# Landmark sums of two batches gated and halved, and a new spacing of the planned attention steps

## The chip, the cores and the metric

One NeuronCore of a Trainium2 chip runs the whole program. Its engines are TensorE (PE, with its weight loads as PEld), VectorE (DVE), ScalarE (ACT), GpSimd (POOL) and the queue of SyncE (SP), which issues DMAs. The metric is the device time of one execution in microseconds; for the kernel before, the median of three runs is 846.47 us (845.29 to 849.52).

## What is computed

A Nystrom attention over 4 batches of 8 heads (576 positions, head size 64, 32 landmarks) feeds two feed-forward layers over 2304 tokens (512 to 2048 to 512).

```
q_lm = q.reshape(B, H, 32, 18, D).mean(axis=3)      # k_lm likewise
A = sm(q, k_lm); Bm = sm(q_lm, k_lm); C = sm(q_lm, k)
Z = Bm.T / (norm1(Bm) * norminf(Bm) + 1e-6)
for _ in range(6):
    Z = 2 * Z - Z @ Bm @ Z
x = A @ Z @ C @ v                 # heads side by side: 2304 x 512
h = x @ w_in1;  x = (h * clip(h + 3, 0, 6) / 6) @ w_out1
h = x @ w_in2;  out = elu(h) @ w_out2
```

The landmark sums are the sums over 18 positions in the first line.

## The kernel before

**Slots.** The first feed-forward layer is cut into 128 slots: 4 batches (b = 0 to 3 in the code, batches 1 to 4 in this text) of 32 slots, each one half of a batch's tokens by one of 16 blocks of the hidden layer. `slot_a1(i)` (line 876) makes the first product of slot i, six matmuls into a tile h (from the tiles ath, atl, nh, nl), then ACT and VectorE make gf from it, ACT gh, and GpSimd or VectorE gl. `slot_a2(i)` (line 906) makes the second product, four groups (one for each dm) of three matmuls into the tiles x. In one turn the first product of slot i and the second of slot i - 3 are made. From slot 32 on a half has 288 tokens. There are two PSUM banks for h, so the h matmuls of slot i + 2 wait until VectorE has read h of slot i.

**Attention.** While the slots of one batch run, the attention of the next is worked in between them, on all engines, as Python generators that give up control after each step: landmark sums (`prep`, line 469, letters p and P for the two groups of heads), score products and their softmax (c: `score_c`, b: `score_b`), the softmax over landmarks (a: `soft`), the iteration for Z (i: `inverse`), the products with v (v, V: `values`), and the end (f: `finish`, with the tiles t0 and Qd on VectorE, a matmul, and a copy; t: `attn_at`). `prep` reduces the tile kt, and then qt into the tile lm, with one VectorE instruction each (128 x 1152 elements to 128 x 64). `score_c` is, in this order: the first half of the products (bk from kt and lm), ACT copies of it into kt, the second half of the products, the row maxima on VectorE in two steps, the exponentials. `inverse` is: VectorE work (BD, BT), two kinds of matmuls, VectorE work that ends with X, then matmuls from X and a VectorE update of X in turn.

**What sets the order.** For batch 2 it is written by hand: in the string PLAN1 (line 1139) each letter s advances the stream of slots by one step (one yield per slot up to slot 15, five per slot from 16 to 35: after the six h matmuls and after each of the four groups), and every other letter one attention step; here each engine's order is the traced one. For batches 3 and 4 it is the string PLAN2 (line 708): `newton(b, at, end)` (line 733) spreads its due times, scaled so that the last is reached at slot `end`, over slots 36 to 56.5 (batch 3) and 64 to 88.5 (batch 4). In the main loop (line 1203) `attend(t)` carries out all steps due up to t, at t = i, and i + 0.2 to i + 0.8 between the groups of slot i. From the end of batch 2's attention on, a scheduler that simulates the program picks the order on each engine by a priority (`wanted`) among what it holds to be ready, so that an engine that it holds to be idle also takes later work. Matmuls of attention (`amm`) and of slots (`smm`) keep their traced order on TensorE through edges. An edge by `after` (so also by `gated`) orders the scheduling alone and is no semaphore on the chip. In the last stage (slots 96 to 127) no attention is left; VectorE and ACT split operands of the second layer there (`load_x`, `load_in2`), and conversions of weights (`conv_out2`, `conv_in2`) run beside the slots throughout.

Of the kernel before, what the change touches and what calls it, by code (L numbers as in the profile page):

```python
# [31 lines left out]
def nystrom_ffn_kernel(ctx: ExitStack, tc, q, k, v, w_in1, w_out1, w_in2, w_out2, out):  # L32
# [117 lines left out]
    def wanted(s):  # L150
        tc.cur_priority = int(1000 * (s + 100))
# [11 lines left out]
    def gated(inst):  # L163
        if gate[0] is not None:
            after(inst, gate[0])
# [84 lines left out]
    def run(gen):  # L250
        for _ in gen:
            pass
# [216 lines left out]
    def prep(b, g):  # L469

        x = kt_t[b, g] = raw_t.pop((b, g, "k"))
        y = qt_t[b, g] = raw_t.pop((b, g, "q"))
        lm = ql_t[b, g] = ap_.tile([128, 2, 32], F32, name="lm", tag="lm", bufs=2)
        for o, i in ((x[:, :, 0:32], x[:, :, 32:]), (lm, y)):
            gated(vec.tensor_reduce(
                out=o, in_=i.rearrange("p r (l c) -> p r l c", c=POOL), axis=AX, op=ALU.add
            ))
            yield 1.3

    def products(ps, w, x, gs):  # L480

# [219 lines left out]
    def newton_tiles():  # L701
# [4 lines left out]
        return EB, sb, sc, cvs  # L706

    PLAN2 = """
        p0 p2 P4 P6 c10 b11 b12 c12.5 c15 c15.5 c16.5 c17.5 i18 i21 i22 i24 i25 a26 a27 i30 i31
        a32 a33 i36 i37 v38 v39 v41 i43.5 i44.5 v45 a45.2 v46 i47 i48 a48.5 V50 V51 V53 a53.5 i55  # L710
        i56 V57 i57.2 a57.5 V58 a59 a60 t60.5 f61 f62 t62.5 f64 f65 t65.5
    """

    def attention(b):
# [18 lines left out]
    def newton(b, at, end):  # L733

        make, gens = attention(b), {}
        plan = PLAN2.split()
        unit = (end - at) / float(plan[-1][1:])
        for x in plan:
            s = at + unit * float(x[1:])
            yield s  # L740
            if x[0] not in gens:
                gens[x[0]] = make[x[0]]()
            wanted(s)
            next(gens[x[0]], None)
        for x in gens.values():
            run(x)
        yield 10 ** 9
# [128 lines left out]
    def slot_a1(i):  # L876
        b, hf, m = i // SB, i // NKT % 2, i % NKT
        nt = span(b, hf)[1]
        ps = banks["h"].tile([128, 512], F32, name="h", tag="h")[:, 0:nt]
        c, o = m // MPC, m % MPC * 128  # L880
        nh, nl = n_t[b, c]
        ath, atl = at_t[b, hf]
        n = 0
        for g in range(G):
            for w, x in ((nh, atl), (nl, ath), (nh, ath)):
                marks["slot"] = smm(ps, w[:, g, o:o + 128], x[:, g, :], n == 0, n == 3 * G - 1).ins
                n += 1
        gf = ft.tile([128, T2], F32, name="gf", tag="gf", bufs=2)[:, 0:nt]
        yield
        act.activation(out=gf, in_=ps, func=AF.Relu, scale=1.0 / 6.0, bias=half_b)  # L890
        yield
        if i < NKT:
            g = gp.tile([128, T2], F32, name="g", tag="gh")[:, 0:nt]
            vec.scalar_tensor_tensor(out=g, in0=gf, scalar=1.0, in1=ps, op0=ALU.min, op1=ALU.mult)
            gt[i] = g, None
            return
        gh = gp.tile([128, T2], F32R, name="gh", tag="gh")[:, 0:nt]
        gl = gp.tile([128, T2], F32R, name="gl", tag="gl")[:, 0:nt]
        vec.scalar_tensor_tensor(out=gf, in0=gf, scalar=1.0, in1=ps, op0=ALU.min, op1=ALU.mult)
        yield  # L900
        act.copy(out=gh, in_=gf)
        yield
        sub(gl, gf, gh.bitcast(F32), vec if i >= NA - 12 else pool)
        gt[i] = (gh, gl)
# [231 lines left out]
                yield  # L1136
            run(a2)

    PLAN1 = "ssssssuulslullslsssspsspssPssPsssoscsbsbcssosccscscsiosssiosissisiosasasssisisasasssisiosvsvososvssisisvasvsisiassVsVsosVassisisVoiasVosasassssosssffftftsssstosnTssnossnosnsssnsTsnosssnsssTssssssss"

    def second_half(slots):

# [60 lines left out]
    for i in range(END, NA):  # L1203
        b, r = i // SB, i % SB

        wanted(i)
        if r == 0:
            run(attn_n(b, NW - 1))
            run(attn_at(b, 1))
            if b + 1 < B:  # L1210
                soon, ready[0] = newton(b + 1, i, i + SB - 7.5), i
            else:
                att.close()
                win.append(ctx.enter_context(tc.tile_pool(name="win", bufs=1, side="right", reuse_waits="tile")))
                xp.append(win[0])
                x0 = load_x(0, vec)
        if b + 1 < B and r in NAT:
            run(attn_n(b + 1, NAT.index(r)))
        if (i - END) % O2 == 0 and conv:
            gate[0] = marks["slot"]  # L1220
            wanted(i + 4)
            conv.pop(0)()
            gate[0] = None
        if i >= NA - SB + XSET:
            wanted(i + 4)
            next(x0, None)
        if i == NA - 14:
            wanted(i + 2)
            load_in2(0)
        attend(i)  # L1230
        a1, a2 = slot_a1(i), slot_a2(i - DELAY)
        next(a1)
        for dm in range(NDM):
            attend(i + (dm + 1) / (NDM + 1))
            next(a1, None)
            next(a2)
        run(a1)
        run(a2)
# [78 lines left out]
```

## Time and profile before

| what | value |
|---|---|
| median of 3 runs | 846.47 us (845.29 to 849.52) |
| profiled execution | 848.42 us |
| its span on the core | 846.6 us |
| TensorE busy | 789.4 us (93%) |
| VectorE busy | 513.9 us (61%) |
| ACT busy | 449.7 us (53%) |
| GpSimd busy | 327.2 us (39%) |
| mean granted clock of TensorE | 0.985 |

In that execution slot 16 starts at 94 us, slot 36 at 172, slot 64 at 267, slot 96 at 367 and slot 127 at 451; the second layer follows. A row of a timeline gives start and duration in us, engine, line, operation, output and inputs by the program's tile names, shapes, a count where like instructions follow each other, and in brackets the idle time of that engine before the row and what ended it. Nearly all rows have line 110, which is the helper that issues every instruction, so tiles tell them apart.

### The profile page before, as it was taken

The numbers are of one execution on the slowest core, as the hardware profiler recorded it, in microseconds if no ns is written. First come the engines' busy times: TensorE is split into PE (matmuls) and PEld (weight loads), VectorE is DVE, ScalarE is ACT, GpSimd is POOL, SyncE is SP. The second block draws the span as 40 slices with busy tenths as digits, with TensorE's granted clock in tenths as the row PEclk, the third lists the DMA queues.
The fourth block names the chain that finished last, engine by engine and source line by source line (L and its number), as shares of the span: only waits on it lengthen the run. The fifth ranks groups of instructions, "written<-read, shape, count | busy, mean of one in ns | idle before, by whom it ended". The sixth has DMA issues, their size and how long they took to land.

```text
span 846.6 us, 15547 instructions
## 1 busy us (share of the span) xinstructions
PE 789.4 (93%) x5740; PEld 687.0 (81%) x5740; DVE 513.9 (61%) x1010; ACT 449.7 (53%) x983; POOL 327.2 (39%) x312
## 2 busy tenths in 40 slices
PE   5699988898999899997999989999999999999998
PEld 2476767687887789877999879898889899898986
DVE  6899756546744764468155877655575545645543
ACT  2687545555656665584456655646544434534433
POOL 0567445544745575455345865331280000000000
PEclk9799999999999999999999999999999999999999
DMA  9957905464868436662162567686763564663531
GB/s 323 404 155 243 302 10 169 129 208 145 284 218 269 156 126 201 204 221 100 42 243 62 168 219 267 233 300 249 240 228 139 176 229 167 235 223 139 195 128 75
DMA packets 96587, 165.64 MB, mean 196 GB/s; under 512 B 7232, under 2 KB 51264, under 8 KB 96512
## 3 DMA queue, kind: packets, MB, share of 16 engines
q1 hardware_dynamic: 96512, 164.66, 56.8%
q8 instruction: 45, 0.74, 0.4%
q14 instruction: 30, 0.25, 0.1%
HBM read 119.54 MB, written 45.09 MB: 194 GB/s over the span
## 4 chain that ended last, share of the span: by engine, by line
PE 58%; DMA 17%; DVE 11%; ACT 5%; issue 4%; POOL 4%; SPq 1%; ACTq 0%; POOLq 0%; DVEq 0%
PE x L110 32%; PE h L110 23%; DMA u<-in_moe_w_out 4%; PE bk L110 4%; DMA u<-in_moe_w_in 3%; DMA ub<-in_moe_w_out 2%; DVE u L110 2%; DVE gf L110 2%; POOL x L110 1%; DVE y L110 1%; POOL xf L110 1%; DMA qt<-in_q 1%; DMA x<-x1d 1%; ACT gf L110 1%; DVE x L110 1%
## 5 line engine op out<-in xcount | busy, mean ns | idle before, releaser
L110 PE MATMUL h<-x,wi 128*128 128x384 f32 x1008 | 205.8, 340 | 4.5 <-DVE u L110 3.7
L110 PEld LDWEIGHTS h<-x,wi 128*128 128x128 f32 x1008 | 181.5, 189 | 19.4 <-DVE u L110 4.9
L110 PE MATMUL x<-gh,wo 128*128 128x288 f32 (+1 forms) x896 | 187.5, 301 | 2.7 <-POOL wo L110 1.9
L110 PEld LDWEIGHTS x<-gh,wo 128*128 128x128 f32 x896 | 142.5, 190 | 17.9 <-issue 8.8
L110 POOL TENSOR_TENSOR gl<-gf,gh 128x288 fp32r<-128x288 f32 (+1 forms) x100 | 85.2, 854 | 116.2 <-ACT gh L110 106.7
L110 ACT CAST gh<-gf 128x288 fp32r<-128x288 f32 (+2 forms) x172 | 78.6, 458 | 82.2 <-DVE gf L110 81.7
L110 PE MATMUL x<-w,gh 128*128 128x512 f32 x360 | 116.6, 394 | 0.5 <-ACT gh L110 0.5
L110 ACT ACTIVATE gf<-y 128x384 f32<-128x384 f32 x96 | 50.4, 525 | 101.4 <-DVE y L110 101.4
L110 DVE SCALAR_TENSOR_TENSOR gf<-gf,y 128x384 f32<-128x384 f32 x96 | 63.3, 660 | 58.6 <-ACT gf L110 58.6
L110 PE MATMUL x<-gl,wo 128*128 128x288 f32 (+1 forms) x448 | 98.1, 295 | 0.6 <-POOL gl L110 0.3
L110 ACT ACTIVATE gf<-h,half_b 128x288 f32<-128x288 f32 (+2 forms) x128 | 63.8, 501 | 65.0 <-PE h L110 55.1
L110 DVE SCALAR_TENSOR_TENSOR gf<-gf,h 128x288 f32<-128x288 f32 (+1 forms) x112 | 49.6, 444 | 73.2 <-ACT gf L110 72.8
L110 PE MATMUL h<-atl,nh 128*128 128x288 f32 (+2 forms) x256 | 82.4, 322 | 8.9 <-DVE gf L110 6.6
L110 PE MATMUL x<-w,ghl 128*128 128x512 f32 x324 | 90.4, 396 | 0.2 <-DVE ghl L110 0.2
L110 PE MATMUL h<-ath,nh 128*128 128x288 f32 (+2 forms) x256 | 76.6, 299 | 0.0
L110 PE MATMUL h<-ath,nl 128*128 128x288 f32 (+2 forms) x256 | 76.6, 299 | 0.0
L110 PEld LDWEIGHTS x<-w,gh 128*128 128x128 f32 x360 | 67.2, 188 | 10.3 <-ACT gh L110 1.0
L110 PEld LDWEIGHTS x<-gl,wo 128*128 128x128 f32 x448 | 73.6, 190 | 1.1 <-POOL gl L110 0.6
L110 PE MATMUL x<-w,gl 128*128 128x512 f32 x180 | 71.0, 395 | 0.0
L110 PEld LDWEIGHTS x<-w,ghl 128*128 128x128 f32 x324 | 60.5, 188 | 9.7 <-DVE ghl L110 0.5
L110 PEld LDWEIGHTS h<-atl,nh 128*128 128x128 f32 x256 | 49.1, 192 | 19.4 <-DVE gf L110 8.4
L110 DVE TENSOR_TENSOR gl<-gf,gh 128x384 fp32r<-128x384 f32 (+1 forms) x72 | 45.9, 637 | 24.1 <-ACT gh L110 20.8
(150 smaller groups left out, 1248.9 us busy)
## 6 DMA issues: line engine op xcount, KB each, us to landing
wi<-wi2p SPq DMA_DIRECT2D x64, 448.0 KB, 5.0
w<-wo2p SPq DMA_DIRECT2D x32, 512.0 KB, 6.1
wi2p<-wi SPq DMA_DIRECT2D x32, 448.0 KB, 3.0
u<-in_moe_w_in SPq DMA_DIRECT2D x25, 512.0 KB, 4.1
w1c<-w1d SPq DMA_DIRECT2D x48, 256.0 KB, 4.7
ub<-in_moe_w_out SPq DMA_DIRECT2D x16, 512.0 KB, 10.2
u<-in_moe_w_out SPq DMA_DIRECT2D x16, 512.0 KB, 5.7
wo2p<-w SPq DMA_DIRECT2D x16, 512.0 KB, 3.4
```

Of the source, the lines that this page charges most:

```text
L110: inst = getattr(self.eng, name)(*a, **kw)
```

## The change

The landmark sums of batches 2 to 4 are made with two instructions in the place of one (one for each half of the tile); batch 1 keeps whole sums. In `newton`, so for batches 3 and 4, a landmark sum gets an edge from the last h matmul of the slot traced last. PLAN2 has eight landmark steps in the place of four and other due times, and its last is 70.5 in the place of 65.5. PLAN1 has eight landmark steps in the place of four and the attention letters at other places; its 108 letters s and the letters o, n and T stand where they stood. A slot in which no planned step is due is traced as all of `slot_a1` and then all of `slot_a2`, in the place of group by group.

```diff
@@ prep @@
         for o, i in ((x[:, :, 0:32], x[:, :, 32:]), (lm, y)):
-            gated(vec.tensor_reduce(
-                out=o, in_=i.rearrange("p r (l c) -> p r l c", c=POOL), axis=AX, op=ALU.add
-            ))
-            yield 1.3
+            for r in [slice(0, 2)] if not b else [slice(0, 1), slice(1, 2)]:
+                gated(vec.tensor_reduce(
+                    out=o[:, r], in_=i[:, r].rearrange("p r (l c) -> p r l c", c=POOL), axis=AX, op=ALU.add
+                ))
+                yield
@@ PLAN2 @@
-        p0 p2 P4 P6 c10 b11 b12 c12.5 c15 c15.5 c16.5 c17.5 i18 i21 i22 i24 i25 a26 a27 i30 i31
-        a32 a33 i36 i37 v38 v39 v41 i43.5 i44.5 v45 a45.2 v46 i47 i48 a48.5 V50 V51 V53 a53.5 i55
-        i56 V57 i57.2 a57.5 V58 a59 a60 t60.5 f61 f62 t62.5 f64 f65 t65.5
+        p0 p1 p2 p3 P4 P5 P6 P7 c10 b11 b12 c12.5 c17 c17.5 c18.5 c19.5 i20 i23 i24 i27 i28 a28.2
+        a29 i33 i34 a34.2 a35 i39 i40 v40.2 v41 v43.5 i46 i47 v47.2 a47.5 v49 i50.5 i51.5 a52
+        V52.2 V53 V55.5 a56 i58 i59 V59.2 i59.4 a60 V61 a61.5 a62.5 t63 f64 f65 t65.5 f69 f70
+        t70.5
@@ newton @@
             wanted(s)
+            gate[0] = marks["slot"] if x[0] in "pP" else None
             next(gens[x[0]], None)
+            gate[0] = None
@@ PLAN1 @@
-    "ssssssuulslullslsssspsspssPssPsssoscsbsbcssosccscscsiosssiosissisiosasasssisisasasssisiosvsvososvssisisvasvsisiassVsVsosVassisisVoiasVosasassssosssffftftsssstosnTssnossnosnsssnsTsnosssnsssTssssssss"
+    "ssssssuulslullslssssppspspsPsPsPsPsssocsbsbcsssoscscscsocisssoisisssoisiaassssisiasassssisoivsvsosovssisivsasvsisisaVsVssVsoasisisViasVsoasoassssssfftosssftsfssstosnTssnossnosnsssnsTsnosssnsssTssssssss"
@@ main loop, slots 36 to 127 @@
         attend(i)
         a1, a2 = slot_a1(i), slot_a2(i - DELAY)
+        if ready[0] > i + 1:
+            run(a1)
+            run(a2)
+            continue
         next(a1)
         for dm in range(NDM):
             attend(i + (dm + 1) / (NDM + 1))
```

## Rows read from the trace of the kernel before

**Rows 1.** The page's list of engines: busy time, share of the span, instructions.
```profile
PE 789.4 (93%) x5740; PEld 687.0 (81%) x5740; DVE 513.9 (61%) x1010; ACT 449.7 (53%) x983; POOL 327.2 (39%) x312
```

**Rows 2.** TensorE's waits over the span: us in total, times, longest.
```profile
PE bk L110 <- DVE Qd L110: 6.4, 2, 3.6
PE bk L110 <- DVE X L110: 5.9, 5, 2.1
```

**Rows 3.** Windows: stretch, length, busy us by engine (count), clock, DMA share, GB/s.
```profile
152.20:155.60 3.40, 3.40 (x28) 2.36 (x27) 2.01 (x3) 1.46 (x4) 1.50 (x3) 0.50 0.00 0
200.00:203.40 3.40, 3.40 (x28) 2.67 (x27) 1.65 (x3) 0.56 (x2) 2.29 (x2) 0.50 0.67 230
398.00:401.30 3.30, 3.30 (x16) 3.30 (x15) 0.91 (x2) 1.70 (x5) 1.89 (x3) 0.50 0.40 153
```

**Rows 4.** Timeline of TensorE: eight matmuls that it waited for.
```profile
102.98 0.97 PE L110 MATMUL bk<-kt,lm 64*32 64x320 f32 x16 [0.53 <-PE x L110]
...
115.99 0.43 PE L110 MATMUL bk<-X 32*32 32x64 f32 x16 [1.43 <-DVE X L110]
...
150.62 0.44 PE L110 MATMUL bk<-Qd,t 128*64 128x128 f32 x4 [3.62 <-DVE Qd L110]
...
187.65 1.28 PE L110 MATMUL bk<-kt,lm 64*32 64x288 f32 x16 [1.64 <-ACT kt L110]
...
199.37 0.43 PE L110 MATMUL bk<-X 32*32 32x64 f32 x16 [2.13 <-DVE X L110]
...
295.07 0.43 PE L110 MATMUL bk<-X 32*32 32x64 f32 x16 [1.48 <-DVE X L110]
...
385.83 0.40 PE L110 MATMUL h<-atl,nh 128*128 128x288 f32 x1 [2.06 <-DVE gf L110]
...
397.63 0.40 PE L110 MATMUL h<-atl,nh 128*128 128x288 f32 x1 [2.49 <-DVE gf L110]
```

**Rows 5.** Timeline of TensorE: matmuls of a slot without a wait.
```profile
372.25 0.69 PE L110 MATMUL x<-gl,wo 128*128 128x288 f32 x4
372.78 0.43 PE L110 MATMUL x<-gh,wo 128*128 128x288 f32 x2
```

**Rows 6.** Timeline of VectorE from 141 us to the end of batch 2's Qd.
```profile
141.18 1.35 DVE L110 TENSOR_REDUCE lm<-qt 128x64 f32<-128x1152 f32 x1 [1.06 <-DMA qt<-in_q]
...
142.59 1.35 DVE L110 TENSOR_REDUCE kt<-kt 128x64 f32<-128x1152 f32 x1
143.86 0.41 DVE L110 SCALAR_TENSOR_TENSOR gf<-gf,h 128x256 f32<-128x256 f32 x1
144.19 0.74 DVE L110 TENSOR_REDUCE st<-ea 128x18 f32<-128x576 f32 x1
...
149.00 1.48 DVE L110 TENSOR_TENSOR Qd<-X,onesbd 128x256 f32<-128x256 f32 x1
```

**Rows 7.** Timeline of ACT: the activation that the gf at 143.86 reads.
```profile
141.58 0.45 ACT L110 ACTIVATE gf<-h,half_b 128x256 f32<-128x256 f32 x1
```

**Rows 8.** Timeline of VectorE: the first and the last of batch 2's four sums.
```profile
97.17 1.35 DVE L110 TENSOR_REDUCE kt<-kt 128x64 f32<-128x1152 f32 x1 [1.11 <-DMA kt<-in_k]
...
101.53 1.35 DVE L110 TENSOR_REDUCE lm<-qt 128x64 f32<-128x1152 f32 x1
```

**Rows 9.** Windows, columns PE, PEld, DVE, ACT, POOL as in rows 3.
```profile
172.00:181.50 9.50, 9.50 (x87) 8.76 (x85) 3.24 (x8) 4.59 (x10) 3.71 (x4) 1.00 0.72 234
260.00:280.00 20.00, 18.02 (x156) 14.97 (x157) 9.69 (x21) 13.63 (x31) 9.88 (x10) 1.00 0.77 253
380.00:400.00 20.00, 15.13 (x104) 14.43 (x103) 18.15 (x31) 8.93 (x20) 11.18 (x11) 0.95 0.28 106
```

**Rows 10.** Timeline of TensorE: h of slot 38, first and last, and of slot 39.
```profile
178.21 0.29 PE L110 MATMUL h<-atl,nh 128*128 128x288 f32 x1
...
180.46 0.29 PE L110 MATMUL h<-ath,nh 128*128 128x288 f32 x1
180.59 0.29 PE L110 MATMUL h<-atl,nh 128*128 128x288 f32 x1
```

More of the change, by code (lines that the diff above doesn't have):

```diff
@@ L1137, in first_half @@
             run(a2)
-    PLAN1 = "ssssssuulslullslsssspsspssPssPsssoscsbsbcssosccscscsiosssiosissisiosasasssisisasasssisiosvsvososvssisisvasvsisiassVsVsosVassisisVoiasVosasassssosssffftftsssstosnTssnossnosnsssnsTsnosssnsssTssssssss"
+    PLAN1 = "ssssssuulslullslssssppspspsPsPsPsPsssocsbsbcsssoscscscsocisssoisisssoisiaassssisiasassssisoivsvsosovssisivsasvsisisaVsVssVsoasisisViasVsoasoassssssfftosssftsfssstosnTssnossnosnsssnsTsnosssnsssTssssssss"
     def second_half(slots):
```

## The prediction

> **What bounds the kernel now.** I read four views. The page's list of engines: TensorE is busy 93% of the span [rows 1], so only time in which it stands still, or runs at its lower clock, can be won. The view of its waits, where those for VectorE's Qd (6.4 us) and X (5.9) come from the attention that this change replans [rows 2]; by stretch, 2.8 us of Qd's and 0.4 of X's lie before 40 us, in batch 1, which is left alone. The view by windows: three stretches of about 3.4 us in which the granted clock was 0.50, that is 1.2 GHz instead of 2.4 [rows 3]. Each follows a wait, of 3.62, 2.13 and 2.49 us; waits of 2.06 and 1.64 were followed by none [rows 4]. TensorE is busy all through such a stretch [rows 3], so it costs half of it, 1.7 us. Then the timelines around the waits, below.
>
> One unit of measure: four matmuls of 128x288 go by in 372.78 - 372.25 = 0.53 us [rows 5], so one takes 0.132 us, the six h matmuls of a slot 0.79, a group of three x matmuls 0.40, a slot 2.37. A planned step due at slot number s runs at the next of the points i (ahead of the h matmuls), i+0.2 (behind them), i+0.4, i+0.6, i+0.8 (between x groups). TensorE keeps the traced order around attention matmuls, so the distance of two points in matmuls is the time that the work between them may take unseen.
>
> **Batch 2's end (Qd).** VectorE runs sums of batch 3 here, two of them, 1.35 us each, at 141.18 and 142.59, and from there works almost without a pause up to the end of Qd at 150.48 [rows 6], for which TensorE waits 3.62 us until 150.62 [rows 4]. The gate holds these sums back to slots 35 to 38, so 2.70 us leave the chain. It can't move up by all of it: its next instruction, at 143.86, needs an ACT result of 142.03 [rows 6, 7], so the gain is about 1.8 us. The order by hand adds to this: the two VectorE steps ahead of Qd's matmuls go 3 stream steps forward (76 for 79) and the softmax sums 2, while the matmuls stay at 79. I take 1.0 us for it, about half of a slot of 256 columns (18 matmuls at 256/288 of 0.132, 2.1 us). The wait falls from 3.62 to 0.8: **-2.8** (bounds 0 and -3.6). With it goes the lower clock of 152.2 to 155.6: **-1.7** (bound 0).
>
> **Batch 2's start.** The first score products stand one stream step earlier (21 for 22). They started at 102.98 [rows 4], 0.10 us after the last sum ended at 101.53 + 1.35 [rows 8]: the wait of 0.53 there is for lm, though the view names PE. The sums can't start earlier, since at 97.17 VectorE waited for the load of k [rows 8]. So the step costs up to one group of x, 0.4, of which I take 0.3, and the halves 0.3 more: a whole sum takes 1.35, a reduction of 576 elements 0.74 [rows 6], so two halves take 1.48, four pairs +0.5, most of it on the path. **+0.6** (bounds 0 and +1.5, two halves late).
> [...]
> The first X matmuls wait 1.43 [rows 4] and stand one step further from their VectorE work (34 to 37, before 34 to 36), three matmuls of 256 columns: **-0.4** (bounds -1.4 and 0).
>
> **Batch 3 (slots 36 to 57).** Here the sums arrive: eight halves of 0.74, 5.9 us. Of the 9.5 us from 172 to 181.5 VectorE is busy 3.24 [rows 9], so 6.3 are free. That holds them, barely. The last half is due at 38.04, so it stands behind the h matmuls of slot 38, the last of which started at 180.46; the first products are due at 38.91, ahead of slot 39 at 180.59 [rows 10]. The last half and its way there take 0.74 and a little: **+0.9**, a new wait for lm (bounds 0, and 2.9 if two or three more halves are late). Queued behind the sums are the slots' gf instructions; those have the time of two slots until an h bank is wanted again, which covers one half but not a row of them.
> The second products waited 1.64 for the kt copies [rows 4]. Copies to products: points 40.0 to 40.8 before, 39.8 to 41.0 after; h and three x groups before (1.98), a slot and an x group after (2.77): **-0.8** (bounds -1.6 and 0).
> The X matmuls waited 2.13 [rows 4]. Their VectorE step stays at point 43.0, they move from 43.6 to 44.0: two x groups, **-0.8** (bounds -2.1 and 0). What is left, 1.3, is less than any wait here that was followed by the lower clock, so the stretch of 200.0 to 203.4 goes: **-1.7** (bound 0).
>
> **Batch 4 (slots 64 to 89).** The same eight halves, taken from between slots 47 and 53, where none ended a wait of more than half a microsecond. Between the last half (66.43) and the products (67.48) a whole slot is left, and VectorE is busy 9.69 of the 20 us from 260 on [rows 9]: **0** (bounds 0 and +2.9). X: points 72.4 and 73.0 become 72.4 and 73.4, 0.79 + 0.40 more; the wait of 1.48 [rows 4] shrinks by **-1.2** (bounds -1.5 and 0).
>
> **Slots traced whole.** No instruction is added or taken away; 7 slots of batch 3, 7 of batch 4 and all 32 of the last stage are traced with h first, then its activation, then the x groups. Today h and x of such a slot mix: slot 38, with no step of its own, has its first h matmul at 178.21 and its last at 180.46 [rows 10]. What TensorE waits for in the last stage is gf, 2.06 and 2.49 us [rows 4]. VectorE is busy there 18.15 of 20 us [rows 9], with work that this edit doesn't touch, and h comes in time now already. **0** (bounds -6.3 and +6.3: those waits and the stretch at the lower clock, gone or once more).
> Steps that issue DMAs (softmax and values load the next batch's q, k and v) move by up to half a slot on SP's queue, earlier for the most part. Nothing waits for these loads, since the sums that read them come later than before; if that cover went, a wait like the one of VectorE at 97.17 (1.11 us [rows 8]) would show. After slot 127 nothing changes.
>
> **Sum**: -2.8 - 1.7 + 0.6 - 0.4 + 0.9 - 0.8 - 0.8 - 1.7 - 1.2 = -7.9 us. The profiled execution took 848.42 (span 846.6); this gives 840.5. It lay 1.95 above the median, so for the median of 846.47 I say **838.5**.
>
> **Rivals.** First, the waits form again (0.25). The order before the last stage comes from a schedule made ahead; the gate is an edge in that schedule and no wait on the chip. If Qd's chain is held by the ACT results ahead of it (gain 0.9, so 2.7 left and the clock still falls: 3.6 less than my terms) and the lm wait of slot 39 is 2.3, the sum is -2.9: 843.6, no change that can be told. For it: the chain does need such a result at 142.03 [rows 7]. If the sums don't move at all, the change not doing what it says, only the plan is left: -1.0 for Qd, and -0.4 - 0.8 - 0.8 - 1.7 - 1.2 + 0.6, so -5.3, which stays inside my forecast.
> Second, slower (0.14): the gated sums lie on the path. Place: slots 36 to 39 and 64 to 67. If the halves run in a row ahead of the slots' gf and the products of both batches wait for all of them, that is 2 x 5.9, and a stretch at the lower clock behind each, 2 x 1.7: +15.2 in place of +0.9, a sum of +6.4, 853. It decides from about three quarters of that on. For it: VectorE has 6.3 us for 5.9 in batch 3 [rows 9]. Against: in batch 4 it has far more, and the gate spreads the halves over three slots.
> Third, a larger gain (0.13): with h first in every slot the last stage's gf comes up to 1.4 us earlier, and its waits and the stretch behind them go, 6.3 more: 832. Against it stands VectorE's load there.
>
> **The numbers.** My forecast has 0.48, from 834 to 842. Within 0.5%, about what a measurement of this kernel can tell from no change, means 842.2 to 850.7. Faster: 0.48 + 0.13 = 0.61; same 0.25; slower 0.14. The range leaves out the far ends of the second and third rivals: 830 to 848, about one in ten on either side.
>
> **What would show it.** Right: no sum of batch 3 or 4 before slot 35's matmuls or slot 63's; Qd's wait near 147 under 1 us; no clock of 0.5 near 152 and 200; X waits of 1.3 and 0.3 in batches 3 and 4; a new wait for lm of about 1 us ahead of slot 39. Wrong: an lm wait over 2 us, gf waits in slots 36 to 40 or 64 to 68, a new stretch at the lower clock, or waits in the last stage that differ by more than 2 us either way.

## The result, and the profile after

The change makes the kernel faster: 834.82 us (median of 4 runs, 833.5 to 838.13) beside 848.0 for the kernel before on the same chip (845.29 to 850.1), a ratio of 0.985 with a 95% interval of 0.981 to 0.990. By the ratio that is about 12.6 us, inside the range that was given, and more than the 7.9 that the sum held. The profiled execution took 838.13 us, the longest of its four, with a span of 836.0, so between the two profiled executions the change is 10.3 us. The page's list of engines after, to be read beside [rows 1]:

```profile
PE 788.2 (94%) x5740; PEld 685.5 (82%) x5740; DVE 504.9 (60%) x1022; ACT 449.2 (54%) x983; POOL 326.1 (39%) x312
```

The number of matmuls is the same and TensorE's busy time almost so; what went is time in which TensorE stood still. The twelve VectorE instructions more are the halves. TensorE's waits after (us in total, times, longest), as [rows 2]:

```profile
PE bk L110 <- DVE lm L110: 11.6, 3, 7.9
PE bk L110 <- DVE Qd L110: 4.1, 2, 2.8
...
PE x L110 <- DVE gl L110: 3.5, 1, 3.5
PE bk L110 <- DVE X L110: 3.2, 4, 1.7
```

Qd is down from 6.4 to 4.1, of which 2.8 is the wait of batch 1 that was there already, and X from 5.9 to 3.2. The single matmuls behind this, in the timeline of TensorE after, as [rows 4]:

```profile
104.28 1.37 PE L110 MATMUL bk<-kt,lm 64*32 64x320 f32 x12 [2.15 <-DVE lm L110]
...
115.39 0.46 PE L110 MATMUL bk<-BD,onesbd 128*128 128x128 f32 x2 [1.46 <-DVE BT L110]
...
150.72 0.44 PE L110 MATMUL bk<-Qd,t 128*64 128x128 f32 x4 [1.29 <-DVE Qd L110]
...
199.17 0.43 PE L110 MATMUL bk<-X 32*32 32x64 f32 x16 [1.71 <-DVE X L110]
...
322.70 0.40 PE L110 MATMUL x<-gh,wo 128*128 128x288 f32 x1 [1.18 <-ACT xs L110]
...
462.45 0.50 PE L110 MATMUL x<-w,gl 128*128 128x512 f32 x1 [3.51 <-DVE gl L110]
```

Two waits at the start of batch 2 are longer: 2.15 for lm (0.53 before) and 1.46 for BT (0.58 before). The one of 1.18 for xs is new. The last row belongs to the start of the second layer; it stands in the place of a wait of 3.67 for u at 486.5 before. The windows of the lower clock after 40 us, with the columns of [rows 3]:

```profile
104.90:108.20 3.30, 3.30 (x17) 1.69 (x13) 1.34 (x6) 0.83 (x2) 0.72 (x1) 0.50 0.29 102
200.50:203.80 3.30, 3.30 (x26) 2.34 (x26) 2.05 (x5) 1.15 (x3) 2.95 (x3) 0.50 0.53 161
463.30:466.60 3.30, 3.30 (x11) 3.02 (x10) 2.06 (x5) 2.05 (x4) 3.05 (x3) 0.50 0.37 144
```

The stretch of 152.2 is gone and one at 104.9 is new, behind the new lm wait; that of 200 stays; that of 397.9 in the last stage is gone; one at 490.1 has become one at 463.3.

To see where the time went, the span of each profile is cut where the first h matmul of a slot starts in the timeline of TensorE. All kernels of this study stand in one table, in us; the ratio is that to the kernel before on the same chip, with its 95% interval. The ratio comes from all executions of a kernel, the four columns from one profiled execution each: after and e5 are the same kernel, and differ by 2.6, 0.1, 1.5 and 0.7. So a difference in a column says little unless it is larger than that or comes back in several kernels.

| kernel | to slot 36 | 36 to 64 | 64 to 96 | 96 to the end | ratio |
|---|---|---|---|---|---|
| before | 171.9 | 95.3 | 99.7 | 479.7 | 1 |
| after | 171.9 | 92.3 | 96.6 | 475.2 | 0.985 (0.981 to 0.990) |
| e5 after, run again | 169.3 | 92.4 | 98.1 | 474.5 | 0.985 (0.981 to 0.988) |
| e1 before + whole slots | 172.9 | 93.1 | 99.4 | 474.7 | 0.993 (0.990 to 0.996) |
| e2 after - whole slots | 168.0 | 92.4 | 100.8 | 477.0 | 0.989 (0.985 to 0.993) |
| e3 after, batch 2 as before | 171.7 | 91.6 | 98.3 | 475.6 | 0.985 (0.981 to 0.989) |
| e4 after - gate | 170.5 | 93.4 | 100.7 | 476.4 | 0.991 (0.988 to 0.995) |
| e6 after, old due times | 168.3 | 94.6 | 95.9 | 475.6 | 0.984 (0.980 to 0.988) |
| e7 after, first products later | 168.5 | 89.8 | 97.6 | 475.3 | 0.981 (0.977 to 0.985) |
| e8 whole in last stage only | 170.2 | 93.2 | 99.5 | 478.0 | 0.992 (0.989 to 0.995) |
| e11 whole before last stage only | 169.6 | 94.5 | 98.5 | 483.5 | 0.990 (0.984 to 0.995) |
| e9 before + x split dealt out | 171.6 | 96.5 | 100.2 | 474.3 | 0.995 (0.992 to 0.998) |
| e10 = e7 + x split dealt out | 167.6 | 93.2 | 97.5 | 470.7 | 0.976 (0.970 to 0.981) |
| e12 = e10 - whole slots | 169.2 | 90.8 | 100.0 | 474.7 | 0.984 (0.981 to 0.987) |

So of the 10.6 us between the spans of before and after 3.0 come from batch 3's slots, 3.1 from batch 4's, 4.5 from the last stage and what follows, and none from batch 2, where most was forecast. A last stage alone (slots 96 to 127) took 83.8 before and 77.7 after; 1.5 of these 6.1 are only moved behind slot 127, since 11 fewer matmuls (at 0.132) lie between the two cuts when slots are traced whole. The rest is waits of TensorE, 5.6 us before and 2.8 after, and the stretch at the lower clock, 1.7 as an estimate (half of its 3.4). The column to the end is free of that move.

### The profile page after: what moved, and what is told of

Read it like the earlier page. It is cut to its first block, busy times and chain, and to the rows that moved or that the text cites. A ratio compares the mean times of both kernels' runs of the same rounds, so it can differ in the third digit from the quotient of the medians.

```text
span 836.0 us, 15555 instructions
## 1 busy us (share of the span) xinstructions
PE 788.2 (94%) x5740; PEld 685.5 (82%) x5740; DVE 504.9 (60%) x1022; ACT 449.2 (54%) x983; POOL 326.1 (39%) x312
## 4 chain that ended last, share of the span: by engine, by line
PE 69%; DMA 9%; DVE 9%; ACT 5%; issue 4%; POOL 3%; SPq 1%; POOLq 0%; DVEq 0%; ACTq 0%
PE x L110 37%; PE h L110 27%; PE bk L110 5%; DMA u<-in_moe_w_out 3%; DMA kt<-in_k 2%; DVE u L110 1%; DMA x<-x1d 1%; DVE gf L110 1%; SPq L110 1%; ACT gf L110 1%; POOL x L110 1%; DVE y L110 1%; DMA x1d<-xs 1%; DVE x L110 1%; DMA u<-in_moe_w_in 1%
## 5 line engine op out<-in xcount | busy, mean ns | idle before, releaser
L110 PE MATMUL x<-gh,wo 128*128 128x288 f32 (+1 forms) x896 | 193.7, 299 | 3.3 <-ACT xs L110 1.2
L110 PEld LDWEIGHTS x<-gh,wo 128*128 128x128 f32 x896 | 145.8, 189 | 13.7 <-issue 4.9
L110 PE MATMUL x<-gl,wo 128*128 128x288 f32 (+1 forms) x448 | 115.0, 294 | 0.1
L110 PEld LDWEIGHTS x<-gl,wo 128*128 128x128 f32 x448 | 79.5, 189 | 0.4 <-POOL gl L110 0.4
## 6 DMA issues: line engine op xcount, KB each, us to landing
ub<-in_moe_w_out SPq DMA_DIRECT2D x16, 512.0 KB, 10.3
```

The lines of the kernel that those rows point to most:

```text
L110: inst = getattr(self.eng, name)(*a, **kw)
```

## The experiments

The first four take the change apart; they ran on one chip and share their runs of the kernel before.

**e1, whole slots alone.** The kernel before with

```diff
@@ main loop @@
+        if ready[0] > i + 1:
+            run(a1)
+            run(a2)
+            continue
```

> The kernel before with one edit, slots without a planned step traced whole. My theory now: the last stage (slot 96 to slot 127) went from 83.8 to 77.7 us because h comes first in each slot, so gf is ready sooner; then this kernel has some 78 us there, no lower clock near 398 us, and takes about 841 (6 to 7 less than before). Rival: the last stage gained because the attention ahead of it left other work behind; then it stays near 84 us here and the time near 848.

Measured: 844.3 us beside 850.56, ratio 0.993 (0.990 to 0.996), about 6 us faster. In the profile 5.0 of it lie between slot 96 and the end. This part was put at nothing, and by itself it gives about half as much as the whole change.

**e2, all but the whole slots.** The kernel after without those four lines.

> The changed kernel with slots traced group by group again, everything else as changed. My theory: the last stage goes back to some 84 us and the time to about 841. Rival (the gain there comes from the attention ahead): 78 us there still, time about 835.

Measured: 841.86, ratio 0.989 (0.985 to 0.993), so 9.3 us by the ratio. The last stage waits for gf as before, here 3.6 us in 96 to 127:

```profile
PE h L110 <- DVE gf L110: 3.6, 2, 2.1
```

With e1: the parts that the sum held for a gain (7.9 forecast) give about 9, and the one held for nothing the rest. The two don't add: 9.3 and 6.0 by themselves are 12.6 together, so on top of the others the whole slots give some 3.3, and the intervals of e2 and after overlap.

**e3, batch 2 as before.** The kernel after with the old PLAN1 and batch 2's sums in one piece; the sums of batches 3 and 4 stay gated.

```diff
-            for r in [slice(0, 2)] if not b else [slice(0, 1), slice(1, 2)]:
+            for r in [slice(0, 2)] if b < 2 else [slice(0, 1), slice(1, 2)]:
...
-    PLAN1 = "ssssssuulslullslssssppspspsPsPsPsPsssocsbsbcsss...
+    PLAN1 = "ssssssuulslullslsssspsspssPssPsssoscsbsbcssoscc...
```

> The changed kernel with the old hand-written order for batch 2 and whole sums for batch 2; gate, new plan and whole slots for batches 3 and 4 stay. My theory: slots 16 to 36 took 77.9 us in both kernels because two things cancel: Qd's wait and its lower clock went (about 4.0), and a new lm wait of 2.15 with a lower clock behind it came (about 3.3), with BT 0.9 later. With the old order the lm wait is 0.5 again and Qd's wait shrinks to about 1.8 by the gate alone, without a lower clock: that stretch takes 74 to 75 us and the time is about 831.5. Rival: the new order is what cured Qd; then its wait is over 3 us here, with a lower clock near 152, and the time about 835.

Measured: 837.91, ratio 0.985 (0.981 to 0.989). Batch 2's end in its timelines, first VectorE, then TensorE:

```profile
147.51 1.48 DVE L110 TENSOR_TENSOR Qd<-X,onesbd 128x256 f32<-128x256 f32 x1
```

```profile
149.13 0.69 PE L110 MATMUL bk<-Qd,t 128*64 128x128 f32 x4 [3.18 <-DVE Qd L110]
```

Qd ends at 148.99, 1.5 us earlier than in [rows 6], close to the 1.8 of the prediction; but TensorE, with less to wait for on the way, also arrives earlier, at 145.95 (149.13 - 3.18) for 147.00, so the wait is 3.18 and not 1.8. Taking the two sums away does not cure this wait; in e1, which has neither the gate nor the new order, it is 3.16. In the kernel after it is 1.29, and the next run says that the order by hand (with the halves) did that. In the time of the whole kernel the new order of batch 2 can't be told: the ratio without it is that of the kernel after.

**e4, no gate.** The kernel after with the edge left out:

```diff
-            gate[0] = marks["slot"] if x[0] in "pP" else None
+            gate[0] = None
```

> The changed kernel without the gate; halves, both plans and whole slots stay. My theory: the sums of batch 3 run again from 131 us on and stand ahead of Qd, whose wait goes from 1.3 to about 2.5 to 3, with a lower clock; those of batch 4 run again in slots 45 to 53. Time 837 to 839. Rival: the gate is worth nothing, since the halves let the other instructions in between: 835.

Measured: 843.45, ratio 0.991 (0.988 to 0.995), so some 5 us of the gain need the gate. The sums of batch 3 stand at 137 to 143 again, and the wait for Qd is 1.29 all the same: with the new order the sums do no harm there. The largest part of the loss shows in batch 4, which takes 100.7 us (96.6 after, 98.1 in e5) with waits of 5.4 us from 262 to 363 (2.3 after), most of them these:

```profile
PE x L110 <- ACT xs L110: 2.4, 2, 1.2
PE bk L110 <- DVE nl L110: 1.5, 1, 1.5
PE bk L110 <- ACT kt L110: 1.1, 2, 0.6
```

The next three, and e8 below, share their runs of the kernel before.

**e5, the kernel after once more**, unchanged.

> The changed kernel once more, unchanged. Theory: the lm wait of 2.15 us and the lower clock at 105 us in its first profile came from a late landing of batch 2's second load of k (9.7 us from issue, 8.3 and 8.6 in the profiles of the kernel before and of the second experiment); in this profile the wait is 1.3 to 1.5 and slots 16 to 36 take 74 to 75 us if the load lands in 8.3 to 8.6 us. Rival: the wait belongs to the new order and is 2 us again, with a lower clock. Time near 835 either way.

Measured: 835.67 beside 849.2, ratio 0.985 (0.981 to 0.988). The ratio repeats; the profile does not in all parts. The second load of k has landed when VectorE comes to its sum, and the first products wait 0.50 (VectorE, then TensorE):

```profile
101.21 0.75 DVE L110 TENSOR_REDUCE kt<-kt 128x32 f32<-128x576 f32 x1
```

```profile
103.71 1.36 PE L110 MATMUL bk<-kt,lm 64*32 64x320 f32 x16 [0.50 <-PE x L110]
```

The lower clock stands at 154.9, 260.7 and 462.1 (after: 104.9, 200.4 and 463.3). Slot 36 starts at 169.3 in the place of 171.9. The profile of after thus caught a late load in batch 2. But the short wait of e5 is the exception: in the other five profiles that have the first products at this step (e2, e4, e6, e8, e11) it is 1.26 to 2.00. The rows of e2 and e8, in the timeline of TensorE (the view names no engine for these waits; the products read lm):

```profile
102.96 1.36 PE L110 MATMUL bk<-kt,lm 64*32 64x320 f32 x16 [1.30 <-issue]
```

```profile
105.22 1.09 PE L110 MATMUL bk<-kt,lm 64*32 64x320 f32 x12 [2.00 <-issue]
```

The second load of k landed 8.6 to 9.7 us after its issue in these five, and 8.1 in e5. With the old order the wait is 0.53 to 0.89 (landings of 7.9 to 8.8). So most of the longer wait belongs to the new order, and how long it is varies with the landing. Even so slot 36 starts sooner with it, as the first column of the table shows: at 171.6 to 172.9 in the four kernels with the old order, at 167.6 to 171.9, with a mean of 169.3, in the ten with the new one.

**e6, old due times.** The kernel after with the due times of the old PLAN2 behind `p0 p1 p2 p3 P4 P5 P6 P7`; gate, halves and batch 2's order stay.

> The changed kernel with the old due times for batches 3 and 4 (the eight landmark halves at 0 to 7, the other steps as before). Theory: the spacing is worth its X and kt waits: slots 36 to 64 have the kt wait of 1.6 and an X wait of 2.1 again, and slots 64 to 96 the X wait of 1.5, so about 94.5 and 98.5 us, and the time is 3 to 4 us over that of the changed kernel. Rival: the spacing is worth nothing beside gate and whole slots; both stretches and the time stay within 1 us of the changed kernel's.

Measured: 835.29, ratio 0.984 (0.980 to 0.988), no different from e5. Batch 3's X wait is what it was:

```profile
195.16 0.43 PE L110 MATMUL bk<-X 32*32 32x64 f32 x16 [2.15 <-DVE X L110]
```

and slots 36 to 64 take 94.6 (92.4 in e5); but 64 to 96 take 95.9 (98.1). The wider spacing shortens the wait that it was forecast to shorten, and nothing is left of that in the total. Two other waits that were put down to the spacing stay short with the old due times: the one for kt in batch 3 is 0.53 (1.64 before), and the X wait of 1.48 in batch 4 is gone here too.

**e7, first products two steps later.** The kernel after with two letters s of PLAN1 moved ahead of batch 2's first products, so that these stand at stream step 23 (21 after, 22 before):

```diff
-    PLAN1 = "...PsPsPsPsssocsbsbcsssoscscscsocisss...
+    PLAN1 = "...PsPsPsPsssosscsbsbcsoscscscsocisss...
```

> The changed kernel with batch 2's first products, their b steps and the kt copies two stream steps later (23, 24, 25, 25 for 21, 22, 23, 23), the second products where they were (27). Theory: two groups of x go ahead of the wait for lm, 0.6 us of fp32 matmuls, so that wait shrinks to 0.7 to 1.5 and no lower clock follows; the time is up to 2 us below that of the changed kernel, unless the second products now wait for kt. Rival: the time of the landing decides and the groups only move from behind the wait to ahead of it while the rest of the chain is late by as much: within 1 us of the changed kernel.

Measured: 833.15, ratio 0.981 (0.977 to 0.985), the lowest ratio so far, though its interval overlaps that of e5. The wait for lm is gone, and smaller ones for the copies of kt come in its place:

```profile
105.97 1.01 PE L110 MATMUL bk<-kt,lm 64*32 64x288 f32 x16 [0.37 <-ACT kt L110]
...
110.90 0.46 PE L110 MATMUL bk<-BD,onesbd 128*128 128x128 f32 x2 [1.22 <-ACT kt L110]
```

**What the whole slots do.** The timeline of VectorE in the last stage, kernel before, from one gf to the next:

```profile
379.06 0.44 DVE L110 SCALAR_TENSOR_TENSOR gf<-gf,h 128x288 f32<-128x288 f32 x1
379.43 1.62 DVE L110 TENSOR_TENSOR x<-u,x 128x384 fp32r<-128x384 f32 x2
380.97 1.16 DVE L110 TENSOR_TENSOR u<-u,x 128x384 f32<-128x384 f32 x1
...
383.46 1.02 DVE L110 TENSOR_TENSOR x<-x 128x384 fp32r<-128x384 f32 x2
384.40 1.01 DVE L110 TENSOR_TENSOR x<-u,x 128x384 fp32r<-128x384 f32 x2
385.34 0.44 DVE L110 SCALAR_TENSOR_TENSOR gf<-gf,h 128x288 f32<-128x288 f32 x1
```

and in the kernel after:

```profile
375.48 0.44 DVE L110 SCALAR_TENSOR_TENSOR gf<-gf,h 128x288 f32<-128x288 f32 x1
375.85 0.54 DVE L110 TENSOR_TENSOR u<-x,u 128x384 f32<-128x384 f32 x1
...
377.25 0.55 DVE L110 TENSOR_TENSOR x<-x 128x384 fp32r<-128x384 f32 x1
377.72 0.44 DVE L110 SCALAR_TENSOR_TENSOR gf<-gf,h 128x288 f32<-128x288 f32 x1
```

The instructions between two gf in these rows are the split of x for the second layer (`load_x`). There are 22 of them in both, but before, the scheduler puts up to 6.7 us of them between two gf (a bunch), and a slot lasts 2.37, with two banks for h; so the h matmuls wait. After, it is at most 5.7, and five of eight are under 3. All of VectorE's work ahead of the gf of slots 98 to 105, mostly this split, the rest `load_in2` and the like, is, slot by slot, 4.9, 0.5, 6.7, 0.8, 3.4, 1.0, 6.1, 0 before and in e2, and 2.3, 5.7, 2.2, 2.8, 0.6, 4.4, 0, 4.7 in after, e1, e5 and e7. That gf itself comes sooner is hardly the reason: from the last h matmul to the end of gf it is 2.33 us in the mean of slots 96 to 125 before and 2.28 after, and from a slot's first h matmul, in slots 106 to 125 where no split of x is left, 2.60 and 2.36, so 0.2 sooner where the third rival had up to 1.4. Two runs then asked which slots must be whole, and three what the bunches cost by themselves.

**e8 and e11, whole in a part only.** The kernel after, whole slots in the last stage alone, or ahead of it alone:

```diff
-        if ready[0] > i + 1:
+        if ready[0] > i + 1 and i >= NA - SB:    # e8
+        if ready[0] > i + 1 and i < NA - SB:     # e11
```

> The changed kernel with slots traced whole only from slot 96 on. Theory: the last stage keeps its 78 us, and slots 36 to 96 lose what whole slots gave at the ends of the batches (nl waits of 0.9 at 262 us where group by group had 2.5, none where it had 1.0 near 358): 191 us and a time of 837 to 838. Rival: whole slots matter in the last stage alone; then slots 36 to 96 take 189 us as in the changed kernel and the time is 835.

> The changed kernel with slots traced whole up to slot 95 only. Theory: what counts is the order that VectorE gets; if its chunks between two gf in slots 96 to 106 come out below 6 us each, the last stage takes 78 to 80 us, and if one is over 6 as in the kernel before, 81 to 84. Rival (h ahead of x in the last stage itself counts): 82 to 84 us whatever the chunks.

Measured: 841.31 in both, ratios 0.992 (0.989 to 0.995) and 0.990 (0.984 to 0.995), each as if no slot were whole (e2: 0.989). For e8 neither expectation held: slots 36 to 96 take 192.7 us, and the last stage 81.2. With whole slots in the last stage only, the bunches are 6.7, 1.6, 5.0, 0 and 7.8 us. With whole slots ahead of it only, they are 4.5, 3.6, 3.6, 1.1, 3.4, 1.0 and 6.1, and the part from slot 96 on takes 483.5, more than I expected by any theory; a stretch of the lower clock at 395.8 and small waits for xs and gh come in there. Part of this belongs to the execution: it took 848.08, 6.8 above the median of its kernel, and from slot 96 on it spends 10.2 us at the lower clock, for 3.4 in after; half of the difference, as an estimate of what it costs, is 3.4 us. The largest bunch, 6.1, is smaller than before, so the size of the bunches alone doesn't give this stretch. Still, the order on VectorE is another one in each of these kernels, and neither half of the whole slots gives the time of both. So the tracing ahead of the last stage matters for where the scheduler puts the split of x within it, and the gain of the kernel after needs both. The third column adds one thing: with gate and new times, slots 64 to 96 take 96.6 to 98.5 in the six kernels in which they are whole, and 99.5 to 100.8 in the three in which they are not (e2, e8, e12).

**e9, the bunches cured by themselves.** The kernel before, with the split of x held by the edge that the gate uses: each of its copies and subtractions is put behind the h matmuls of the slot before it.

```diff
@@ load_x @@
-                xt_t[t, kk, i] = h[i].bitcast(F32R), l[i].bitcast(F32R)
-                to_pair(f, *xt_t[t, kk, i], eng)
+                a, b = xt_t[t, kk, i] = h[i].bitcast(F32R), l[i].bitcast(F32R)
+                gated(act.copy(out=a, in_=f))
+                gated(sub(b, f, a.bitcast(F32), eng))
...
-            sub(f[1], f[0], l[0], eng)
+            gated(sub(f[1], f[0], l[0], eng))
@@ main loop @@
+            gate[0] = marks["slot"]
             next(x0, None)
+            gate[0] = None
```

> The kernel before with one edit: the ACT and VectorE work that splits x for the second layer (load_x, 22 VectorE instructions in the last stage) gets the same edge to the slot traced last that the change gives the landmark sums. Slots are traced group by group, as before. Theory after eight runs: the last stage is set by how many of these instructions stand between two gf of the slots on VectorE (before: 4.9, 0.5, 6.7, 0.8, 3.4, 1.0, 6.1 us; changed kernel: 2.3, 5.7, 2.2, 2.8, 0.6, 4.4, 0, 4.7), and whole slots helped by dealing them out more evenly. With one or two per slot the gf waits of 2.06 and 2.49 and the lower clock go without whole slots: 76 to 78 us for slots 96 to 127 where 83.8 were, some 6 us off the time. Rival: h ahead of x is what counts; then this stays within 2 us of 83.8.

Measured: 847.02 beside 850.46, ratio 0.995 (0.992 to 0.998): 3.4 us by the medians, where some 6 were expected. (e9 to e11 share their runs of the kernel before, e12 has its own.) The split now runs from 378 to 436 in the place of 375 to 397, mostly 0.6 to 1.6 us of it between two gf, and the part from slot 96 to the end is 474.3, for 479.7: about what whole slots give there (474.7), without whole slots. The last stage takes 78.3, and the gf waits of 2.06 and 2.49 are gone, with 0.94 and 0.61 in their place. The profiled execution took 844.38, 2.6 below the median of its kernel, so the 5.4 of this column may be more than most executions gain. The stretches ahead of it differ from before by -0.3, +1.2 and +0.5, which is within what two executions of one kernel differ by there (after and e5: 2.6, 0.1 and 1.5).

**e10, both.** e7 with the split of x held as in e9.

> The kernel of experiment seven (changed kernel, first products of batch 2 later) with the same edge on the splitting of x. Theory: its last stage of 78.5 us, with a gf wait of 2.2 and a lower clock, comes to 75 to 76, and the time 2 to 3 us under that of experiment seven, unless the later stores of x meet the first quartets. Rival (h ahead of x counts, and it is had already): no change.

Measured: 830.55 us, ratio 0.976 (0.970 to 0.981): the lowest of the study, though its interval overlaps that of e7. VectorE in its last stage:

```profile
366.08 0.46 DVE L110 SCALAR_TENSOR_TENSOR gf<-gf,h 128x288 f32<-128x288 f32 x1
366.46 0.57 DVE L110 TENSOR_TENSOR u<-u,x 128x384 f32<-128x384 f32 x1
368.42 0.46 DVE L110 SCALAR_TENSOR_TENSOR gf<-gf,h 128x288 f32<-128x288 f32 x1 [1.39 <-ACT gf L110]
368.79 0.61 DVE L110 TENSOR_TENSOR u<-x,u 128x384 f32<-128x384 f32 x1
```

and the window of slots 96 to 127:

```profile
358.40:432.30 73.90, 73.90 (x566) 73.84 (x560) 44.20 (x86) 44.54 (x103) 36.46 (x36) 1.00 0.48 166
```

VectorE does what the scheduler gave it in small pieces and then waits for ACT, and TensorE does not stand still once in the stage.

**e12, e10 without whole slots.** This asks whether whole slots were only another way to break up the bunches.

> The kernel of experiment ten with slots traced group by group again. Theory: with x dealt out by the edge, the last stage needs no whole slots and stays at 74 to 76 us; what whole slots still give are the ends of batches 3 and 4 (waits for nl and gf of 1 to 2 us in sum), and what they cost is the wait for gl of 3.6 us at the start of the second layer, in whose place the wait for u of 3.7 us comes back some 30 us later, with 1 us less around it. So 829 to 832, beside some 830. Rival: whole slots are worth their 3 to 6 us for themselves; then the last stage takes 78 us or more and the time is 834 to 837.

Measured: 836.91 beside 851.89, ratio 0.984 (0.981 to 0.987), some 7 us behind e10. With the bunches gone the last stage still waits 2.3 us, in four pieces:

```profile
PE h L110 <- DVE gf L110: 1.5, 2, 0.9
PE x L110 <- DVE gl L110: 0.8, 2, 0.4
```

and takes 78.9 for 74.0; from slot 96 to the end it is 474.7 for 470.7. So the rival of the expectation holds: whole slots are not only another way to break up the bunches. By the ratios the split dealt out gives some 0.5% without whole slots (e9) and some 0.5% with them (e10 beside e7), and whole slots 0.8% on top of it (e10 beside e12) and 0.7% by themselves (e1); the intervals, 0.3 to 0.6% to either side, leave room in all of these. The last column, one profile each, is less plain: 479.7 before, 474.7 with whole slots, 474.3 with the split dealt out; among the changed kernels 477.0 with neither (e2), 475.3 with whole slots (e7), 474.7 with the split dealt out (e12) and 470.7 with both (e10). What whole slots do beyond breaking up the bunches was not taken further apart. That h first, and so an earlier activation, gives the later steps of a slot more time would fit, but it is argued only.

## Why the prediction was right, and where it was not

- **Total and sign: right, in part by luck.** 838.5 was said, 834.8 measured. The parts that were given a gain gave 9.3 (e2) for 7.9; the part that was put at nothing gave the rest. But two of the parts that it was made of, the new order of batch 2 and the wider spacing (-4.5 in the sum), can't be told in the time: without the one (e3) and without the other (e6) the ratio stays 0.985 and 0.984, where the intervals would hide some 3 us. What can be told is the gate (some 5 us, e4), though not through the wait that it was priced for, and the whole slots (3.3 to 6.0). By stretch, forecast and measured:

| stretch | forecast | after - before | mean of like profiles |
|---|---|---|---|
| to slot 36 | -4.3 | 0.0 | -2.6 (new order, ten) |
| 36 to 64 | -2.4 | -3.0 | -3.1 (gate and new times, nine) |
| 64 to 96 | -1.2 | -3.1 | -1.9 (those also whole, six) |
| 96 to the end | 0 | -4.5 | -4.5 (after, e3, e5, e6, e7) |

- **Batch 2's end, -2.8: size nearly right (-2.3), cause wrong.** The wait fell from 3.62 to 1.29. The prediction gave 1.8 of it to the sums that leave and 1.0 to the order. e3 shows the first as small (3.18 left), because the wait is the difference of two arrivals and TensorE's came forward with VectorE's; e4 shows the second, with the halves, as all of it. The chain ahead of Qd in the kernel after:

```profile
145.07 0.36 DVE L110 SCALAR_TENSOR_TENSOR gf<-gf,h 128x256 f32<-128x256 f32 x1
147.68 0.42 DVE L110 SCALAR_TENSOR_TENSOR gf<-gf,h 128x256 f32<-128x256 f32 x1 [2.24 <-ACT gf L110]
...
149.08 1.49 DVE L110 TENSOR_TENSOR Qd<-X,onesbd 128x256 f32<-128x256 f32 x1
```

VectorE is idle for 2.24 us there, for an ACT result: the first rival's mechanism, and the reason why Qd still ends at 150.57.

- **Batch 2's start, +0.6: the right way, and undersized.** The lm wait rose by 1.6 in the profile of after, just over its bound of 1.5, not at all in e5, and by 0.7 to 1.5 in the five others with this placement; the mean of the seven is 0.9. The sums of batch 2 after, VectorE's timeline, beside [rows 8]:

```profile
97.36 1.41 DVE L110 TENSOR_REDUCE kt<-kt 128x32 f32<-128x576 f32 x2 [1.08 <-DMA kt<-in_k]
...
101.77 0.75 DVE L110 TENSOR_REDUCE kt<-kt 128x32 f32<-128x576 f32 x1 [1.57 <-DMA kt<-in_k]
...
103.43 1.40 DVE L110 TENSOR_REDUCE lm<-qt 128x32 f32<-128x576 f32 x2
```

The second load of k landed 9.7 us after its issue in this profile (8.3 before, 8.6 in e2) and VectorE waited 1.57 for it (in e8 a landing of 9.7 again, with an lm wait of 2.00). The sentence that nothing waits for loads held for batches 3 and 4, not here. Two halves behind each other take 1.41, for 1.35 whole, so 0.06 and not the 0.13 that was taken. Two halves that stand by themselves, at 0.74 to 0.75 each, take 0.13 to 0.15 more than a whole sum. X fell by 1.0 (forecast 0.4), and a wait for BT rose by 0.9, which the prediction had not seen.

- **Batch 3, +0.9 - 0.8 - 0.8 - 1.7: sum near (-3.0 for -2.4) by luck, terms not.** The lm wait did not come. Half of the sums ran ahead of slot 36 (171.9), the first of them, at 168.84, ahead of slot 35's matmuls (170.31) too; the gate orders the schedule and holds nothing back on the chip:

```profile
168.84 0.74 DVE L110 TENSOR_REDUCE kt<-kt 128x32 f32<-128x576 f32 x1
...
170.71 1.40 DVE L110 TENSOR_REDUCE lm<-qt 128x32 f32<-128x576 f32 x2
...
175.99 1.40 DVE L110 TENSOR_REDUCE kt<-kt 128x32 f32<-128x576 f32 x2
...
178.63 0.74 DVE L110 TENSOR_REDUCE lm<-qt 128x32 f32<-128x576 f32 x1
```

The last half ends at 179.37, and the h matmuls of slot 39 start at 182.29. So the place of the slower rival was never full. The kt wait went whole (1.64, forecast 0.8); among the nine kernels with gate and new times it is 0 to 0.55 but for e8, where 1.35 is left, and with the old due times (e6) it is 0.53, so the spacing alone is not what takes it away. X gave 0.4 for 0.8: 1.70 to 1.75 is left in all nine. The stretch at the lower clock behind it stayed in after, e8, e10 and e11, and is absent from e2, e3, e5, e7 and e12.

- **Batch 4, -1.2: too small.** The X wait of 1.48 went, though not by the spacing alone, since it is gone in e6 too, with the old due times; the gate's worth (e4) and that of whole slots both show in this stretch, which the prediction had not foreseen; a new wait of 1.18 for xs took a part back.

- **Slots traced whole, 0: the step that failed.** The sentence was that VectorE is busy there "with work that this edit doesn't touch". The work is the same, its places are not: the scheduler, given another traced order, dealt out the split of x in other pieces, and the bunches of it are what gf, and so the h matmuls, wait for (e9: dealt out by an edge alone, without whole slots, most of these waits go too). This is shown for part of the gain; what whole slots give beside it (e12) is open. The third rival had the place and the waits (those for gf, [rows 4]) right. Its size of 6.3 is near the 6.0 of e1, but on top of the rest it is some 3.3, and gf waits of 2.8 us stay in the last stage after. Its way was another: gf comes 0.2 sooner in a slot, not 1.4, and it has less ahead of it on VectorE.

- **The lower clock as a price for a wait.** Two of the three stretches were to go, one with a wait that was to fall to 0.8, one because a wait of 1.3 was shorter than any that had one behind it. (Before had a fourth, at 490.1, that the prediction doesn't count.) In the profile of after one followed the X wait of 1.71 and one the lm wait of 2.15, in e5 one stands at 154.9, behind waits of 1.30 for Qd and of 0.57 and 0.76 for weights. That reason falls. Between 40 us and the last microseconds each profile has three to five such stretches, whatever was cured (before four, after three), so the -3.4 of these terms were not earned as forecast; other waits that went made up for them.

- **The signs.** Of the signs of being right, the profile of after has no lower clock near 152 and no X wait over 0.3 in batch 4. The others did not come: Qd's wait is 1.29 (under 1 was said), that for X in batch 3 is 1.71 (1.3), a stretch at the lower clock stands at 200, there is no lm wait ahead of slot 39, and a sum of batch 3 ran ahead of slot 35. Three signs of being wrong came: an lm wait over 2 us, though in batch 2, a new stretch at the lower clock (104.9), and waits in the last stage that differ by 2.8 us. So the time was inside the range while most of the ways to it were not those of the prediction.

What stays open: why the gate is worth some 5 us in the total when the waits that it was meant for are cured without it (e4); it shows as waits in batch 4, and no run took those apart. The halves were not run by themselves.

## What to carry to other kernels

Where a scheduler made ahead fills the idle time of an engine, look at what lies between two instructions that a critical engine waits for: the share of busy time says nothing of bunches, and an edge that ties each piece of filler to a slot took some 0.5% off the time here (e9). An edit of the traced order can move all filler behind it, so "work that this edit doesn't touch" should not be priced at nothing in such a kernel. A wait is the difference of two arrivals: freeing the producer shortens it only by what the consumer doesn't gain from the same change (e3: Qd 1.5 us earlier, the wait for it 0.4 shorter).

## What the runs showed of the hardware

The same program had the lower clock (granted 0.50) at 104.9, 200.4 and 463.3 in one execution and at 154.9, 260.7 and 462.1 in another. The X wait of batch 3 was 1.71 in one with a stretch behind it, and 1.74 in the other without. In all nine kernels with gate and new times that wait is 1.70 to 1.75, and four of the nine have the stretch behind it. In these traces the length of a wait alone doesn't tell whether the clock falls behind it.

What the lower clock does to matmuls can be read where they follow each other without a wait. Before, in the stretch that begins at 397.9:

```profile
398.29 0.44 PE L110 MATMUL h<-atl,nh 128*128 128x288 f32 x1
398.53 0.44 PE L110 MATMUL h<-ath,nl 128*128 128x288 f32 x1
398.77 0.44 PE L110 MATMUL h<-ath,nh 128*128 128x288 f32 x1
```

They start 0.24 us apart, 1.2 columns in a ns, which is where the prediction's 1.2 GHz shows in the trace; its 2.4 is twice that, by the granted 0.50. At the full clock the same matmuls start 0.132 apart [rows 5], 2.2 columns in a ns, so not quite twice as fast, and a stretch of 3.4 us costs some 1.5 as an estimate, a little under the half that is taken for it above.

A subtraction of 128x384 on VectorE took 0.54 to 0.57 us in most of the rows above, but one took 1.16 and two together 1.62 in the bunch of the kernel before, where GpSimd made two gl beside them:

```profile
379.65 2.07 POOL L110 TENSOR_TENSOR gl<-gf,gh 128x288 fp32r<-128x288 f32 x2 [2.70 <-ACT gh L110]
```

In the last stages of all fourteen profiles there are 308 of these subtractions. The 137 that no GpSimd instruction overlaps took 0.54 to 0.56 us each. Of the 171 that overlap one, 57 took as little and 114 took 0.61 to 1.67. So none was slow without GpSimd at work, as far as the rough spans of GpSimd in a profile tell. It can also be GpSimd that is slow: in the kernel after the subtractions at 376.78 and 377.25 take 0.55, and the gl beside them 1.79 us, for 0.83 in the next one. No run took the GpSimd work away, so that it is the cause is not shown.

```profile
376.66 1.79 POOL L110 TENSOR_TENSOR gl<-gf,gh 128x288 fp32r<-128x288 f32 x1 [3.86 <-ACT gh L110]
378.71 0.83 POOL L110 TENSOR_TENSOR gl<-gf,gh 128x288 fp32r<-128x288 f32 x1 [0.26 <-ACT gh L110]
```
